# First quarter of a fused attention and feed-forward kernel: block widths 480, 512, 512, 416, single weight issues, tile 0 in three pieces, engine orders written out

## Chip, cores and metric

The kernel runs on one core of a Trainium2 chip. The metric is the device time of one execution in microseconds (us), the median over several runs. The profiler's times count from the first instruction of the program.

## What is computed

x has 2048 rows of 640 numbers, all in float32. Each row is normalised; from it come an attention branch, with 32 heads of 20 over a window of 8 positions two apart, and a feed-forward branch of width 1536.

```python
xn = _layernorm(x)                                  # x: (1, 2048, 640)
qkv = (xn @ wqkv).reshape(B, S, 3, 32, 20)          # wqkv: (640, 1920)
idx = pos[:, None] - off[None, :]                   # off = arange(8) * 2
logits = einsum("bhsd,bhswd->bhsw", q, k[idx]) * 20 ** -0.5   # masked where idx < 0
s = einsum("bhsw,bhswd->bhsd", softmax(logits), v[idx]).reshape(B, S, 640) @ wo
g = silu(silu(xn @ w1) @ w2)                        # w1: (640, 1536), w2: (1536, 640)
out = x + s * g
```

## The kernel before

The 2048 rows are worked on in four groups of 512 (half of the sequence, even or odd rows), each of four tiles of 128 rows. For every group TensorE runs the QKV product, then (from the second group on) the output projection of the group before, then the feed-forward part; after the last group comes its output projection. To keep float32 accuracy every operand is split into a high part, rounded to the matmul's float32r, and a low part, the remainder; a product of a 128-row slice is three matmuls: high by high, low by high, high by low. In the code these are TH and TL for the activations, and wh and wl for the weights; a product (k, c) is k = 0 for TH by wh, 1 for TL by wh, 2 for TH by wl, on the 128-row slice c of 5.

The QKV columns (1920) are worked on in four blocks, called quarters after their eight heads: block q has BQ = 192 columns of Q (64 in the last) beside 160 of K and 160 of V, so 512, 512, 512 and 384 columns. A block for a group is 5 slices by 4 tiles by 3 matmuls, 60 in all. Blocks 2 to 4 and all later groups go slice by slice over the four tiles (L735 to L749). The first block of the first group is special, since nothing is loaded then: `first_quarter` (L629) writes its order out by hand. It warms TensorE up with 22 transposes of the identity, and then interleaves, tile by tile, the turning of x (`turn`, transposes on TensorE, high part on ACT, low part on DVE) with lists of products (`products`). `begin` (L640) makes the statistics of a tile (two halves, an aggregate), the root on ACT (L461), the reciprocal (L463) and the scaling (L652), which for tile 0 is cut in two pieces of 384 and 256 columns.

Weights come by `raw_load` (L360), which for a QKV block issues two DMAs, the Q columns (L384) and the K and V columns (L385), on the queue of SyncE (SP). `w_load` (L397) splits them: the high part on ACT (L418, here called wh0 for block 0 of the weight units, and so on), the low part on GpSimd or, for the units named in ON_DVE, on DVE (L421, wl0 and so on). The split halves go to a ring of seven slots (WR) and are also stored to DRAM (L427), from where later groups load them again (L410). x tile t is loaded by `load_x` (L447); the first tile comes in two halves (L693).

Each engine runs its instructions in the order in which the program has them. That order is made by a planner, the class Weave: every operation is added with an engine, a duration, what it reads and writes, and a priority; `order` (L139) simulates the engines with these durations and takes, for each engine but TensorE, the ready operation that can start first, by priority among equals. TensorE's order is that of the program text. The planner has constants for the landing of a DMA (LAND, EARLY, RATE), for the load of an activation table (TABLE), and a rule, `held_back` (L115), by which ACT puts off an operation that would delay a silu that is due. SP's order in the start follows priorities: the weight unit k has 1 + k, and the tiles 1 to 3 of x have X_AT.

## Time and profile before

| | us |
|---|---|
| median of 3 runs | 619.84 (619.4 to 620.7) |
| the profiled execution | 619.89 |
| its span, first to last instruction | 618.1 |
| TensorE busy in the span | 612.7 (99%) |
| VectorE (DVE) busy | 561.5 (91%) |
| ScalarE (ACT) busy | 309.1 (50%) |
| GpSimd (POOL) busy | 112.6 (18%) |

The page gives the busy time of each engine, the chain of work that ended last and the costliest groups of instructions; PE is TensorE's matmuls and PEld its weight loads, which overlap them. A matmul's duration in the trace includes its way through the array, so that the rate of a row of matmuls is read from their starts, or from a stretch that holds a known number of them. What the numbers of the rows mean is said where they are used.

### The profile page before, as it was taken

The page shows a single profiled execution, that of the slowest core. Times are in us where ns is not written, and L with a number is a line of the kernel's source. Part 1 is how long each engine was busy: PE and PEld are TensorE (multiplying, and loading weights), DVE is VectorE, ACT ScalarE, POOL GpSimd, SP SyncE. Part 2 cuts the span into 40 slices and gives each one's busy share as a digit, 9 for nine tenths or more (in the row PEclk, how much of TensorE's full clock was granted, in tenths as well). Part 3 has the DMA queues.
Part 4 walks back from the last instruction along what each step waited for, and adds up shares of the span by engine and source line. Part 5 has one row for each costly group of instructions (what it writes and reads, how often), then busy time and mean ns, then how long its engine had stood idle before and what let it go on. Part 6 is the DMA issues. An engine that isn't in the chain of part 4 may idle for free.

```text
span 618.1 us, 9090 instructions
## 1 busy us (share of the span) xinstructions
PE 612.7 (99%) x3357; PEld 553.6 (90%) x3357; DVE 561.5 (91%) x581; ACT 309.1 (50%) x651; POOL 112.6 (18%) x168
## 2 busy tenths in 40 slices
PE   8999999999999999999999999999999999999997
PEld 7889899998889999999888999999988999999997
DVE  6558999999989998999998999999979999899974
ACT  5435548937376313951944502583396316153650
POOL 4510000011101133111222233311121213311100
PEclk9999999999999999999999999999999999999999
DMA  8999999875999998764699999955579999966642
GB/s 254 339 282 332 368 355 394 331 239 178 296 325 350 343 357 256 240 195 142 190 254 244 332 338 308 281 180 163 160 204 283 245 327 289 309 192 197 206 131 105
DMA packets 65449, 162.45 MB, mean 263 GB/s; under 512 B 7053, under 2 KB 29165, under 8 KB 65405
## 3 DMA queue, kind: packets, MB, share of 16 engines
q0 software_dynamic: 20016, 82.58, 44.3%
q1 hardware_dynamic: 45389, 79.29, 40.7%
q8 instruction: 26, 0.43, 0.3%
q14 instruction: 18, 0.15, 0.1%
HBM read 109.55 MB, written 34.16 MB: 232 GB/s over the span
## 4 chain that ended last, share of the span: by engine, by line
PE 99%; DVE 0%; ACT 0%; issue 0%; POOL 0%; POOLq 0%
PE acc L774 22%; PE acc L777 15%; PE acc L746 10%; PE acc L745 10%; PE acc L747 10%; PE rot L894 9%; PE rot L895 9%; PE rot L893 9%; PE acc L684 2%; PE rot L635 1%; PE rot L777 1%; PE rot L774 0%; PE rot L662 0%; PE acc L875 0%; ACT w L418 0%
## 5 line engine op out<-in xcount | busy, mean ns | idle before, releaser
L747 PE MATMUL acc<-w,thl 128*128 128x512 f32 (+1 forms) x300 | 112.4, 375 | 0.0
L746 PE MATMUL acc<-w,thl 128*128 128x512 f32 (+1 forms) x300 | 112.4, 375 | 0.0
L745 PE MATMUL acc<-w,thl 128*128 128x512 f32 (+1 forms) x300 | 112.4, 375 | 0.0
L774 PE MATMUL acc<-w,sh 128*128 128x384 f32 x384 | 111.7, 334 | 0.0
L777 PE MATMUL acc<-w,sh 128*128 128x256 f32 x384 | 107.1, 279 | 0.0
L899 ACT ACTIVATE sh<-rot 128x512 fp32r<-128x512 f32 x48 | 28.7, 597 | 155.6 <-PE rot L895 155.4
L895 PE MATMUL rot<-thl,w 128*128 128x512 f32 x240 | 93.8, 391 | 0.0
L894 PE MATMUL rot<-thl,w 128*128 128x512 f32 x240 | 93.8, 391 | 0.0
L893 PE MATMUL rot<-thl,w 128*128 128x512 f32 x240 | 93.5, 389 | 0.0
L579 DVE TENSOR_TENSOR pr<-q,kv 128x2560 f32<-128x2560 f32 x32 | 90.2, 2817 | 1.3 <-DMA kv<-kv 1.1
L617 DVE TENSOR_TENSOR pr<-e,kv 128x2560 f32<-128x2560 f32 x32 | 90.3, 2823 | 0.7
L582 DVE TENSOR_REDUCE l<-pr 128x128 f32<-128x2560 f32 x32 | 90.0, 2813 | 0.5
L622 DVE TENSOR_TENSOR pr<-pr 128x1280 f32<-128x1280 f32 x64 | 74.0, 1156 | 1.5
L774 PEld LDWEIGHTS acc<-w,sh 128*128 128x128 f32 x384 | 72.1, 188 | 1.1
L777 PEld LDWEIGHTS acc<-w,sh 128*128 128x128 f32 x384 | 72.2, 188 | 0.9
L410 POOL DMA_DIRECT2D w<-half_w x72 | 38.5, 534 | 189.1 <-PE acc L777 64.4
L410 POOL DMA_DIRECT2D w<-half_q x52 | 27.6, 531 | 238.8 <-DVE thl L480 91.0
L745 PEld LDWEIGHTS acc<-w,thl 128*128 128x128 f32 x300 | 56.3, 188 | 8.7
L747 PEld LDWEIGHTS acc<-w,thl 128*128 128x128 f32 x300 | 56.3, 188 | 8.7
L746 PEld LDWEIGHTS acc<-w,thl 128*128 128x128 f32 x300 | 56.3, 188 | 8.6
L774 PE MATMUL acc<-w,thl 128*128 128x384 f32 x225 | 63.1, 333 | 0.0
L495 ACT ACTIVATE xin<-sf 32x256 f32<-32x256 f32 (+1 forms) x144 | 54.6, 379 | 9.6 <-DVE sf L522 7.9
(92 smaller groups left out, 1044.5 us busy)
## 6 DMA issues: line engine op xcount, KB each, us to landing
w<-half_w POOLq DMA_DIRECT2D x72, 640.0 KB, 6.2
w<-half_q POOLq DMA_DIRECT2D x39, 512.0 KB, 4.6
half_w<-w SPq DMA_DIRECT2D x24, 640.0 KB
w<-half_wo POOLq DMA_DIRECT2D x15, 640.0 KB, 5.6
kv<-kv SPq DMA_DIRECT2D x15, 560.0 KB
half_q<-w SPq DMA_DIRECT2D x15, 512.0 KB
kv<-kv SPq DMA_DIRECT2D x15, 420.0 KB
gate<-in_B_w_dram SPq DMA_DIRECT2D x16, 320.0 KB
```

Source lines behind the costliest of these rows:

```text
L579: dve(2560, lambda t=t: nc.vector.tensor_tensor(out=PR, in0=win(qq[:, t:t + 2, :], W, 0), in1=win(kv[:, 0, t:t + 2, :], W, CQ), op=OP.mult ...
L582: dve(2560, lambda t=t: nc.vector.tensor_reduce(out=l[:, t:t + 2].rearrange("p t w h -> p (t w h)"), in_=PR.rearrange("p t w (h d) -> p (t ...
L617: dve(2560, lambda t=t, v=v: nc.vector.tensor_tensor(out=PR.rearrange("p t w (h d) -> p t (w h) d", d=DH), in0=e[:, t:t + 2].rearrange("p ...
L622: dve(2 * k * CQ, lambda k=k: nc.vector.tensor_tensor(out=PR[:, :, 0:k, :], in0=PR[:, :, 0:k, :], in1=PR[:, :, k:2 * k, :], op=OP.add), [] ...
L745: nc.tensor.matmul(o, hi, wh, start=c == 0, stop=False)
L746: nc.tensor.matmul(o, lo, wh, start=False, stop=False)
L747: nc.tensor.matmul(o, hi, wl, start=False, stop=c == DC - 1)
L774: nc.tensor.matmul(a[t][0][:, :CA], st, w[:, :CA], start=first, stop=last)
L777: nc.tensor.matmul(b[t // 2][0][:, h * CB:(h + 1) * CB], st, w[:, CA:], start=first and h == 0, stop=last, skip_group_check=True)
L893: nc.tensor.matmul(h, wh[:, cs], TH[i][:, c, :], start=c == 0, stop=False)
L894: nc.tensor.matmul(h, wh[:, cs], TL[i][:, c, :], start=False, stop=False)
L895: nc.tensor.matmul(h, wl[:, cs], TH[i][:, c, :], start=False, stop=c == DC - 1)
```

## The change

The Q columns are cut 160, 192, 192, 96, so that the blocks have 480, 512, 512 and 416 columns. A block of the first quarter then has three equal pieces of 160 columns and comes by one DMA in place of two. A pair of halves of under 512 columns is laid out with the second half at column 512, and its store and loads name the two halves. Tile 0 of x is scaled and turned in pieces of one, two and two slices. The warm-up has 18 transposes. The lists of products are written in one string, FIRST, and orders for ACT, DVE and GpSimd in ORDER; `chain` makes each named operation of an engine wait in the plan for the one before it (a name that stands under an engine which does not run it is passed over). In FIRST, T is a turn, with the pieces if any are named; 0h1 is tile 0, high by high, slice 1; x is low by high, and w high by low. In ORDER, q and r are a tile's root and reciprocal, s its statistics, g its aggregate, a its scaling, h and l its high and low parts (tile, piece). The subtractions for the weight units 0, 3 and 8 are on DVE, where 2, 3 and 4 were. Tiles 1 to 3 of x get the places 2.5, 4.5 and 6.5 among the weight units. The planner's landing times for early DMAs are changed, and `held_back` counts a table load also for operations without a table when the loaded table is not silu's.

```diff
-BQ = 192
+QC = 160, 192, 192, 96
+QO = 0, 160, 352, 544
+PAIR = 512
-WARM, WARM2 = 22, 3
+WARM, WARM2 = 18, 3
-X_AT = 2, 7, 8
-TILE_AT = 1, 1.5, 2, 2.5
+X_AT = 2.5, 4.5, 6.5
-ON_DVE = (2, 3, 4)
+ON_DVE = (0, 3, 8)
+FIRST = """T00 T01 0h0 T02 0h1 0x0 0x1 0h2 0h3 0x2 0w1 0w2 T1 0w0 0x3 0x4 1h0 0h4 1h2 1h34 0w4 0w3 1x0
+           1x1 1x2 1w3 1w4 1x4 T2 1w01 1x3 2w0 1h1 2h4 2h3 2w1 1w2 2h01 2h2 T3 2x0 2x123 2w3 3w012 2w4
+           3h4 3w34 3h0123 3x01234 2w2 2x4"""
+ORDER = {"ACT": """q0 wh0 wh1 h00 h01 wh2 h02 wh3 q1 wh4 h10 h11 q2 h20 h21 q3 h30 h31 wh5""",
+         "DVE": """wl2 s0a s0b g0 r0 a00 a01 a02 s1b s1a l00 l01 g1 l02 r1 a10 wl3 s2b s2a l10 g2 s3a
+                   l11 r2 a20 s3b g3 r3 a30 l20 l21 l31 l30""",
+         "POOL": """wl1 wl0 wl4 wl5"""}
...
-    EARLY = 10.0, 0.6
+    EARLY = 5.5, 1.45
...
                 if o.table is not None and o.table != "silu":
                     need += self.TABLE * (1 + (o.table != table)) + (self.GATE if gate else 0)
+                elif table != "silu":
+                    need += self.TABLE
...
+    def chain(self):
+
+        for e, names in ORDER.items():
+            row = [self.named[n] for n in names.split() if n in self.named and self.named[n].eng == e]
+            for a, b in zip(row, row[1:]):
+                a.users.append(b)
+                b.left += 1
+
     def order(self):
+        self.chain()
...
-                o.end = dma + self.LAND + o.late + (self.EARLY[1] if lanes[e][-1] and t < self.EARLY[0] else 0.0)
+                o.end = dma + (self.EARLY[1] if t < self.EARLY[0] else self.LAND) + o.late
...
     def width(u):
-        return qcols(u[1]) + 2 * CQ if u[0] == "q" else D
+        return QC[u[1]] + 2 * CQ if u[0] == "q" else D
...
+    def both_of(r, n):
+        if n < PAIR:
+            return r[:, :2 * PAIR].rearrange("p (k m) -> p k m", k=2)[:, :, :n]
+        return r[:, :2 * n].rearrange("p (k m) -> p k m", k=2)
...
             def go():
-                nc.sync.dma_start(r[:, :w], all3[:, 0, q * BQ:q * BQ + w])
+                if w == CQ:
+                    nc.sync.dma_start(r.rearrange("p (s m) -> p s m", s=3), all3[:, :, q * CQ:(q + 1) * CQ])
+                    return
+                nc.sync.dma_start(r[:, :w], all3[:, 0, QO[q]:QO[q] + w])
                 nc.sync.dma_start(r[:, w:].rearrange("p (s m) -> p s m", s=2), all3[:, 1:, q * CQ:(q + 1) * CQ])
...
-            add("POOL", 1.0, lambda: nc.gpsimd.dma_start(both, src), [("half", u)], [kh, kl], due + 10,
+            add("POOL", 1.0, lambda: nc.gpsimd.dma_start(both, src.rearrange("p (k m) -> p k m", k=2)), [("half", u)], [kh, kl], due + 10,
...
-        PARTS = (0, 3), (3, DC)
+        PARTS = ((0, 1), (1, 3), (3, DC)), ((0, 3), (3, DC))
...
-        turn(0)
-        pe(0.11 * WARM2, lambda: warm(WARM2, ACC[5]), [], [("acc", 5)])
-        products(0, [(0, 0), (1, 0), (0, 1), (1, 1), (2, 0), (0, 2), (1, 2)])
-        turn(1)
-        products(0, [(2, 1), (0, 3), (1, 3), (2, 2)])
-        products(1, [(0, 0), (0, 1), (0, 2)])
...
+        for step in FIRST.split():
+            if step[0] == "T":
+                turn(int(step[1]), [int(j) for j in step[2:]] or (0, 1))
+                turned[0] = 1
+                continue
+            t, k, cs = int(step[0]), "hxw".index(step[1]), step[2:]
+            products(t, [(k, int(c)) for c in cs], 0.1 * turned.pop(0))
```

## Rows read from the trace of the kernel before

**Rows 1.** The page: busy time, share, count by engine; the chain's shares by engine.
```profile
PE 612.7 (99%) x3357; PEld 553.6 (90%) x3357; DVE 561.5 (91%) x581; ACT 309.1 (50%) x651; POOL 112.6 (18%) x168
...
PE 99%; DVE 0%; ACT 0%; issue 0%; POOL 0%; POOLq 0%
```
**Rows 2.** Waits of TensorE, whole span: for whom, us in total, times, longest.
```profile
PE rot L635 <- POOL ident masks.py:199: 1.4, 1, 1.4
PE acc L684 <- ACT w L418: 0.2, 1, 0.2
```
**Rows 3.** Busy by stretch: us, PE PEld DVE ACT POOL, clock, DMA share, GB/s.
```profile
24.00:37.60 13.60, 13.60 (x61) 11.26 (x60) 7.92 (x16) 4.87 (x12) 8.92 (x6) 1.00 1.04 287
...
51.20:61.60 10.40, 10.40 (x61) 10.40 (x60) 8.77 (x10) 6.28 (x14) 0.00 (x0) 1.00 1.07 367
```
**Rows 4.** Timeline of TensorE's matmuls: start, duration, engine, line, operation, shapes, count.
```profile
7.46 1.89 PE L684 MATMUL acc<-w,thl 128*128 128x512 f32 x5
...
10.12 0.75 PE L662 MATMUL rot<-ident,xin 128*128 128x128 f32 x5
10.62 4.81 PE L684 MATMUL acc<-w,thl 128*128 128x512 f32 x20
...
24.00 0.39 PE L745 MATMUL acc<-w,thl 128*128 128x512 f32 x1
```
**Rows 5.** Timeline of TensorE's weight loads for the warm-up transposes.
```profile
1.38 4.55 PEld L635 LDWEIGHTS rot<-ident 128*128 128x128 f32 x22 [1.38 <-POOL ident masks.py:199]
...
6.83 0.36 PEld L635 LDWEIGHTS acc<-ident 128*128 128x128 f32 x3
```
**Rows 6.** Timeline of DVE in the first quarter; in brackets idle time and releaser.
```profile
4.84 0.80 DVE L652 TENSOR_SCALAR xin<-xin,mv,sd 128x384 f32<-128x384 f32 x2
6.26 0.49 DVE L647 BATCH_NORM_STATS2 st<-xin 128x6 f32<-128x320 f32 x1 [0.61 <-DMA xin<-in_A_x_dram]
7.44 0.56 DVE L670 TENSOR_TENSOR thl<-rot,thl 128x384 fp32r<-128x384 f32 x1 [0.69 <-ACT thl L666]
...
9.21 0.83 DVE L652 TENSOR_SCALAR xin<-xin,mv,sd 128x640 f32<-128x640 f32 x1
...
12.61 0.88 DVE L647 BATCH_NORM_STATS2 st<-xin 128x6 f32<-128x320 f32 x2
...
14.62 0.61 DVE L652 TENSOR_SCALAR xin<-xin,mv,sd 128x640 f32<-128x640 f32 x1
```
**Rows 7.** The same timeline, ACT and GpSimd.
```profile
6.19 1.27 POOL L421 TENSOR_TENSOR w<-pr,w 128x512 fp32r<-128x512 f32 x1 [2.97 <-ACT w L418]
...
8.68 0.29 ACT L461 ACTIVATE sd<-mv,epst 128x1 f32<-128x1 f32 x1 [0.34 <-DVE mv L648]
```
**Rows 8.** The same timeline, issues on SP's queue.
```profile
1.67 0.43 SPq L384 DMA_DIRECT2D pr<-in_A_wqkv_dram  x1
...
2.62 0.47 SPq L447 DMA_DIRECT2D xin<-in_A_x_dram  x1
```
**Rows 9.** Busy by stretch before 7.46; the last two columns are DMA share, GB/s.
```profile
1.40:3.25 1.85, 1.85 (x9) 1.85 (x10) 0.22 (x3) 0.84 (x2) 1.82 (x1) 1.00 0.64 195
3.25:4.50 1.25, 1.25 (x8) 1.25 (x7) 1.00 (x3) 0.18 (x1) 0.00 (x0) 1.00 0.67 148
4.50:5.90 1.40, 1.40 (x8) 1.40 (x7) 0.96 (x3) 0.53 (x2) 0.00 (x0) 1.00 1.04 352
5.90:7.46 1.56, 1.53 (x11) 1.29 (x9) 0.51 (x2) 0.75 (x3) 1.27 (x1) 1.00 1.01 280
```
**Rows 10.** The page: a costly group (mean ns) and DMA issues (us to landing).
```profile
L617 DVE TENSOR_TENSOR pr<-e,kv 128x2560 f32<-128x2560 f32 x32 | 90.3, 2823 | 0.7
...
w<-half_q POOLq DMA_DIRECT2D x39, 512.0 KB, 4.6
```
**Rows 11.** Timelines of DVE and of TensorE's weight loads at the last projection's start.
```profile
598.63 1.29 DVE L480 TENSOR_TENSOR thl<-xin,thl 128x512 fp32r<-128x512 f32 x2 [2.22 <-ACT thl L479]
...
600.97 0.19 PEld L774 LDWEIGHTS rot<-w,thl 128*128 128x128 f32 x1
```

More of the change, by code (lines that the diff above doesn't have):

```diff
@@ L59 @@
 class Op:
-    __slots__ = ("eng", "dur", "fn", "prio", "lock", "table", "nbytes", "late", "seq", "left", "users", "ready", "start", "end")
+    __slots__ = ("eng", "dur", "fn", "prio", "lock", "table", "nbytes", "late", "seq", "left", "users", "ready", "start", "end", "lag")
 class Weave:
@@ L84, in __init__, with add @@
         self.writer, self.readers = {}, {}
-    def add(self, eng, dur, fn, reads=(), writes=(), prio=0.0, lock=False, table=None, nbytes=0, late=0.0):
+        self.named = {}
+    def add(self, eng, dur, fn, reads=(), writes=(), prio=0.0, lock=False, table=None, nbytes=0, late=0.0, name=None, lag=0.0):
         o = Op()
-        o.late = late
+        o.late, o.lag = late, lag
+        if name:
+            self.named[name] = o
         o.eng, o.dur, o.fn, o.prio, o.lock, o.table, o.nbytes = eng, dur, fn, prio, lock, table, nbytes
@@ L198, in order @@
                 u.left -= 1
-                hop = self.HOP if u.eng != e or o.nbytes else 0.0
+                hop = self.HOP if u.eng != e or o.nbytes else -o.lag
                 if u.eng == "ACT" and e == "DVE" and u.prio > 0:
@@ L294, in local_attention_silu_ffn, with dve, act, pe @@
     po = lambda n: 0.11 + n * 0.0023
-    def dve(n, fn, reads, writes, prio, lock=False):
-        add("DVE", dv(n), fn, reads, writes, prio, lock)
-    def act(n, fn, reads, writes, prio, table=None):
-        add("ACT", ac(n), fn, reads, writes, prio, table=table)
-    def pe(dur, fn, reads, writes):
-        add("PE", dur, fn, reads, writes)
+    def dve(n, fn, reads, writes, prio, lock=False, name=None):
+        add("DVE", dv(n), fn, reads, writes, prio, lock, name=name)
+    def act(n, fn, reads, writes, prio, table=None, name=None):
+        lag = 0.09 if name else 0.0
+        add("ACT", ac(n) - lag, fn, reads, writes, prio, table=table, name=name, lag=lag)
+    def pe(dur, fn, reads, writes, lag=0.0):
+        add("PE", dur, fn, reads, writes, lag=lag)
         clock[0] += dur
@@ L404, in w_load @@
         r = WR[s]
-        both = r[:, :2 * n]
+        both = both_of(r, n)
         kh, kl = ("wh", s), ("wl", s)
@@ L421, in w_load @@
         add(eng, cost, lambda: by.tensor_tensor(
-            out=r[:, n:2 * n], in0=raw, in1=r[:, :n].bitcast(F32), op=OP.subtract), [kh] + kr, [kl],
-            due if pool_does else LOW_AT if k < LO else 50, lock=True)
+            out=both[:, 1], in0=raw, in1=r[:, :n].bitcast(F32), op=OP.subtract), [kh] + kr, [kl],
+            due if pool_does else LOW_AT if k < LO else 50, lock=True, name=f"wl{k}")
         if what[i] == "store":
@@ L426, in w_load @@
             halves[u] = kept
-            dma(lambda: nc.sync.dma_start(kept, both.bitcast(F32)), [kh, kl], [("half", u)], 2 * n * P * 4,
+            dma(lambda: nc.sync.dma_start(kept.rearrange("p (k m) -> p k m", k=2), both.bitcast(F32)), [kh, kl], [("half", u)], 2 * n * P * 4,
                 due + STORE)
@@ L438, in w_next @@
         s, n = i % RING, width(want)
-        return WR[s][:, :n], WR[s][:, n:2 * n], ("wh", s), ("wl", s)
+        both = both_of(WR[s], n)
+        return both[:, 0], both[:, 1], ("wh", s), ("wl", s)
     def w_done(n=1):
@@ L448, in load_x @@
             [("xin", u) for u in range(t, t + n)], n * P * D * 4, clock[0] if prio is None else prio,
-            late=LATE if g else 0.4 * t)
+            late=LATE if g else 0.0)
     def ln_stats(t, after=()):
@@ L457, in ln_stats, with ln_rstd @@
         dve(60, lambda: nc.vector.bn_aggr(out=MV[:, t, :], in_=st), [ks + (0,), ks + (1,)], [("mv", t)], 1)
-    def ln_rstd(a, b, at=1, after=()):
+    def ln_rstd(a, b, at=1, after=(), name=None):
         n = range(a, b)
         act(b - a, lambda: nc.scalar.activation(SD[:, 0, a:b], MV[:, a:b, 1], AF.Sqrt, bias=epst, scale=1.0),
-            [("mv", t) for t in n] + list(after), [("sd", t) for t in n], 0, "sqrt")
+            [("mv", t) for t in n] + list(after), [("sd", t) for t in n], 0, "sqrt", name=name and "q" + name)
         dve(10, lambda: nc.vector.reciprocal(out=SD[:, 1, a:b], in_=SD[:, 0, a:b]),
-            [("sd", t) for t in n], [("rs", t) for t in n], at)
+            [("sd", t) for t in n], [("rs", t) for t in n], at, name=name and "r" + name)
     def ln_apply(t):
@@ L671, in turn, with products @@
                     out=TL[i][:, a:b, tsl(t)], in0=v, in1=TH[i][:, a:b, tsl(t)].bitcast(F32), op=OP.subtract),
-                    [kp] + t_keys(i, range(a, b), [t], ["th"]), t_keys(i, range(a, b), [t], ["tl"]),
-                    1.6 if a and not t else 0)
-        def products(t, steps):
+                    [kp] + t_keys(i, range(a, b), [t], ["th"]), t_keys(i, range(a, b), [t], ["tl"]), 0, name=f"l{t}{j}")
+        def products(t, steps, more):
             o, kp = ps[t]
@@ L683, in products @@
                 given[t] = given.get(t, 0) + 1
-                pe(mm(512), lambda x=x, c=c, w=w, first=first, last=last: nc.tensor.matmul(
-                    o, x[i][:, c, tsl(t)], w, start=first, stop=last), [(kx, i, c, t), kw], [kp])
-        def passes(*ks):
-            return [(k, c) for k in ks for c in range(DC)]
+                pe(mm(480) + more, lambda x=x, c=c, w=w, first=first, last=last: nc.tensor.matmul(
+                    o[:, :w.shape[1]], x[i][:, c, tsl(t)], w, start=first, stop=last), [(kx, i, c, t), kw], [kp])
+                more = 0.0
         given = {}
```

63 lines of the change are left out of this document (29 added, 34 removed).

## The prediction

> **What bounds the kernel now.** First read the busy shares and the chain on the page: TensorE is busy 99% of the span, and the chain that ended last is TensorE throughout [rows 1]. Then ask what TensorE waited for: in the whole span the list has two waits, 1.4 us for the identity at the start and 0.2 us for a weight split, and nothing later [rows 2]. Then see what a matmul costs where nothing waits: 60 matmuls of 512 columns take 13.60 us (0.2267 each), 60 of 384 take 10.40 (0.1733 each) [rows 3]. The difference is 0.0534 us for 128 columns, so 0.0133 for 32. From 24.00 on the kernel is a string of such matmuls without a gap; that part can only change with its columns, or get a new wait. So the change must earn its time before 24.00, in the first quarter [rows 4]: tile 0's first product starts at 7.46, seven products are done by 10.12, where tile 1's transposes begin, and from there 53 products and 15 transposes run almost closed to 24.00: 10.12 + 53 x 0.2267 + 3 groups of transposes at 0.50 (10.12 to 10.62) = 23.63, which leaves 0.37 for small gaps.
>
> So the end of the kernel hangs on two numbers: when tile 1's transposes start (T1, now 10.12), and how many products are done by then.
>
> **The profiled execution** took 619.89 us with a span of 618.1; the median of the three runs is 619.84. I count within the span and carry the sum to the median; the two stand 0.05 apart.
>
> **Widths.** In groups 1 to 3, 60 products of 480 gain 60 x 0.0133 = 0.80 us and 60 of 416 give it back: nil. In group 0 the last block pays the same 0.80, but the first quarter earns only on what runs behind T1, as products before it lie beside waits: 51 x 0.0133 = 0.68. Net 0.12 slower. 480 and 416 lie between measured widths, so I take them on their line. A reader who looks at the first quarter alone books 0.7 us that the last block takes back.
>
> **One issue per weight block.** A block of the first quarter is two issues on SP's queue; two of them take it from 1.67 to 2.62 [rows 8]. With one, five steps of 0.47 fall away, 2.3 us of queue, and the x tiles move past weights on it: x1 goes behind blocks 0 and 1 (was behind 0), x2 behind 3 (was behind 5), x3 behind 5 (was behind 6). The queue then has x1 at 2.6 as now, x2 near 4.0, block 4 near 4.5. But an issue is not a landing. The DMA engines are busy 0.67 of 3.25 to 4.50, at 148 GB/s, and full from 4.50 on, at 352 and then 280 GB/s [rows 9]. Only the first stretch had room: filling it gives (148/0.67 - 148) x 1.25 = 91 KB, or at 280 GB/s 165 KB. Moved by 5.90 are 195 x 1.85 + 148 x 1.25 + 352 x 1.40 = 1039 KB, so 1130 to 1204 with the change. How far use lags behind: x1 is used at 6.26 [rows 6], when 1039 + 0.36 x 280 = 1140 KB had moved; up to and with x1, 917 KB were asked for; the lag is 223 KB. In the new order x1 stands at 1145 KB, block 2 at 1390, block 3 at 1635, block 4 at 2208 (245 KB a block, 328 a tile). At 280 GB/s from 5.90: x1 at 6.5 to 6.8, block 2 at 7.4 to 7.6, block 3 at 8.2 to 8.5, block 4 at 10.3 to 10.6. Bounds: with 352 GB/s held, x1 6.4, block 3 7.8, block 4 9.4; with nothing gained, 7.1, 8.8 and 10.9. I take 7.4, 8.3 and 10.3 for the blocks.
>
> The Trainium skill, page "DMA: Bandwidth & Descriptors", section "Issuing engines are not separate DMA queues", says that the sequencer time saved on issuing is usually small beside the transfer itself. From 4.50 on the trace agrees, from 3.25 to 4.50 (0.67) it does not. By that rule alone the issues saved would be worth nothing: the third case below.
>
> **Orders of DVE and ACT up to T1.** T1 needs x1, its two statistics, the aggregate, the root on ACT (q1), the reciprocal and the scaling (a10). Now the second statistic waits behind tile 0's subtraction of 7.44, the root comes at 8.68, right behind the aggregate, the scaling at 9.21 to 10.04 [rows 6, 7]. The new DVE order has both statistics first (0.88 for such a pair at 12.61), then the subtractions l00 and l01, 0.25 and 0.42 by the 0.56 of 384 columns: the aggregate is done 1.8 us behind x1, at 8.5. But the new ACT order has q1 behind the split of block 3, and this split waits for its landing: 8.3 + 0.55 = 8.85. From root to T1 there are 10.12 - 8.68 = 1.44 us, with a scaling of 0.83; the same scaling took 0.61 at 14.62, so T1 comes 1.22 to 1.44 behind 8.85, at 10.07 to 10.29; with block 3 at its bounds, 9.6 and 10.8. I take the low end, 10.0.
>
> Queued behind q1 on ACT are the split of block 4 and then h10, tile 1's high half. Block 4 at 10.3 puts h10's end near 11.3; TensorE comes to its product 1h0 at T1 + 0.50 + 3 x 0.2133 = 11.1. This new wait costs 0.2; with block 4 at its bounds, 0 and 0.5.
>
> Subtractions change engines: blocks 0 and 3 on DVE, 1, 2 and 4 on GpSimd, at 1.27 each [rows 7]. Block 2 at 7.4 is split by 8.0 and subtracted by 9.3; its product is the last before T1 and ends at 9.6. That is 0.4 of cover; with block 2 at 8.0 the cover is gone and T1 0.2 later. Block 0's, now on DVE without a fixed place, is wanted only behind T1; ahead of the scaling it would cost up to 0.6. I take 0.
>
> **Three pieces of tile 0, warm-up of 18.** The scaling starts at 4.84 as now, in three pieces; the warm-up ends 0.85 earlier, so the first transpose can go near 5.25 and the first product near 6.4, against 7.46. That gives room for nine products before T1, against seven: 2 x 0.2267 = 0.45 us that is no longer run behind it. The earlier start gives nothing besides: 0x0 needs l00 (7.7), and the queue is in order.
>
> The clock: the weight loads of the 22 warm-up transposes come every 0.207 us, those of the three at 6.83 every 0.12 [rows 5]: the lower level (1.2 GHz), then the higher (2.4), though the clock column of [rows 3] says 1.00. TensorE had run without a gap until then; in the new kernel it has gaps from 5.3 to 6.4. If the rise comes later but before T1, the four products behind block 3's split take 0.2 more each: 0 to 0.8. I take 0.
>
> The skill's page "TensorE: Matmul & The Clock Gate", Part 4, has it that transposes do not release the clock. Here it rose after nothing but transposes. By the rule the four cut ones could not matter, by the trace they could.
>
> **Layout and planner.** Stored blocks of 480 and 416 become two runs in place of one. Such loads land 4.6 us after issue [rows 10], seven slots of 2.7 us ahead; doubled it would be hidden still: 0. The rule that holds ACT's copies back for a table load can move any copy of the later groups; ACT is busy 50% [rows 1]. No wait of TensorE there can go, as there is none: 0, or the last rival.
>
> **Sum.** T1 0.12 earlier, two products 0.45, widths -0.12, h10 -0.2, and 0.15 of the 0.37 of gaps, as x2 and x3 come some 3 us sooner (tile 2's statistics are at 12.61 now): 0.4 us. 619.84 - 0.4 = **619.4**. Its own range: T1 at 9.6 and no wait, 0.52 + 0.45 - 0.12 + 0.15 = 1.0, 618.8; T1 at 10.7 and a wait of 0.5, 0.6 slower, 620.4.
>
> **The rivals.** Larger gain, **618.3** (617.9 to 618.6): single issues hold 352 GB/s, block 3 lands by 7.5, q1 goes right behind the aggregate (8.1), T1 is at 9.3, h10 does not wait, the gaps are gone: 0.82 + 0.45 - 0.12 + 0.37 = 1.5. For it: the engines reached that rate once [rows 9]; against it: they were full at 280 afterwards. Chance 0.22.
>
> Nothing gained, **619.9** (619.6 to 620.3): issue was no bound, block 3 comes at 8.8, T1 at 10.5; the two products make good what that costs: -0.38 + 0.45 - 0.12. For it: share 1.01 at 5.90 [rows 9]; against it: the idle third before. Chance 0.12.
>
> Slower, **621.2** (620.3 to 622.5): the later groups are planned anew and the last join breaks. The last two subtractions of the turned attention output run from 598.63 to 599.92; the weight load that needs the second stands at 600.97 [rows 11], 1.05 us of room. DVE is busy 91% [rows 1]. One of its 2.8 us operations [rows 10] put ahead of that chain leaves TensorE standing 2.8 - 1.05 = 1.75 us: less 0.4, 1.35 slower. It decides once the chain comes 1.05 us later against TensorE. Against it: the chain follows TensorE's own results, so a common shift leaves the room. Chance 0.13.
>
> **How the numbers follow.** Forecast 0.53, rivals 0.22, 0.12 and 0.13. A measurement of this kernel can tell about 0.2%, 1.24 us, from no change: faster is below 618.60, slower above 621.08. Faster takes the larger gain and 0.03 of the forecast's edge, 0.25; slower takes 0.08 of the last rival and 0.02 of a late clock, 0.10; the same has 0.65. The range, 618.0 to 621.0, leaves out some 0.07 below and 0.11 above.
>
> **What would show it.** The second quarter's first product near 22.8 (24.00 now); group 0's last block 11.2 us long (10.40 now); T1 near 10.0, behind block 3's split and q1 on ACT; h10 behind block 4's split. T1 before 9.5 shows the larger gain, a wait of TensorE after 24 the last rival, products spaced 0.4 apart after 7.5 the late clock. Wrong from the ground would be blocks of 480 and 416 off the line of [rows 3].

## The result and the profile after

The changed kernel takes 622.68 us (median of 20 runs, 620.47 to 623.66), the kernel before 619.82 (20 runs, 619.26 to 623.40): ratio 1.0033 [1.0023, 1.0043], slower by 0.33% or 2.1 us (the ratio goes by the means; the medians lie 2.9 apart), where 0.4 us faster was forecast and 621.0 was the top of the range. The profiled execution of after took 623.66 us with a span of 621.9, against 619.89 and 618.1; it is the slowest of its twenty. Executions of one kernel lie up to 4 us apart here, so verdicts come from ratios with their intervals, and single profiles are asked for mechanisms.

TensorE's timeline of after, to be held against [rows 4] (start, duration, what it waited for in brackets):

```profile
6.75 0.48 PE L715 MATMUL acc<-w,thl 128*128 128x480 f32 x1 [0.75 <-ACT thl L698]
...
7.21 0.46 PE L715 MATMUL acc<-w,thl 128*128 128x480 f32 x1
9.32 3.17 PE L715 MATMUL acc<-w,thl 128*128 128x480 f32 x7 [1.65 <-DVE thl L702]
12.29 1.27 PE L694 MATMUL rot<-ident,xin 128*128 128x128 f32 x5
...
26.46 0.40 PE L770 MATMUL acc<-w,thl 128*128 128x512 f32 x1
```

The first product comes 0.7 sooner than before, nine are done ahead of tile 1's transposes as planned, and yet T1 is at 12.29 (10.12 before) and the second quarter at 26.46 (24.00). Busy by stretch, columns as in [rows 3] (the granted clock is the third from the end):

```profile
7.70:9.30 1.60, 0.00 (x0) 0.00 (x0) 1.11 (x4) 0.41 (x1) 0.13 (x1) 0.78 1.08 368
9.30:12.29 2.99, 2.97 (x8) 2.35 (x9) 2.58 (x8) 1.78 (x5) 1.61 (x2) 0.50 1.08 338
12.29:17.70 5.41, 5.41 (x22) 4.76 (x21) 3.04 (x10) 2.14 (x6) 0.81 (x1) 0.71 0.96 295
17.70:26.50 8.80, 8.80 (x48) 7.60 (x46) 2.46 (x6) 4.08 (x12) 2.96 (x3) 1.00 1.01 314
...
53.71:64.91 11.20, 11.20 (x61) 11.18 (x60) 10.69 (x13) 7.30 (x16) 0.00 (x0) 1.00 1.06 329
147.30:160.30 13.00, 13.00 (x62) 11.25 (x61) 12.90 (x10) 12.43 (x30) 1.60 (x3) 1.00 0.68 196
160.30:173.90 13.60, 13.60 (x61) 11.25 (x60) 13.39 (x13) 5.41 (x14) 1.76 (x3) 1.00 1.04 351
```

Two things are to be seen. TensorE stands idle from 7.70 to 9.30, the clock falls, and the products up to T1 run at half of it (the lower level, 1.2 GHz), 0.4 us apart. And 60 products of 480 columns take 13.00 us, not the 12.80 of the line; 416 take 11.20, as on it. The span's 3.8 us are then accounted for: 26.46 - 24.00 = 2.46 in the first quarter, 11.20 - 10.40 = 0.80 in group 0's last block, and three times 13.00 + 11.20 - 13.60 - 10.40 = 0.20 in groups 1 to 3, together 3.86. The last term is the roughest: from block start to block start it is 0.12 a group, and elsewhere the later groups move by up to 0.4 us either way, which nearly cancels. TensorE has one later wait, the second of these, at a feed-forward product:

```profile
PE acc L715 <- DVE thl L702: 1.6, 1, 1.6
...
PE acc L799 <- DVE sl L926: 0.2, 1, 0.2
```

DVE and ACT say why 0x0 starts at 9.32. Tile 0's low part (L702) stands behind tile 1's statistics (L674) in the written order, and these wait 1.71 us for tile 1's x:

```profile
8.19 0.89 DVE L674 BATCH_NORM_STATS2 st<-xin 128x6 f32<-128x320 f32 x2 [1.71 <-DMA xin<-in_A_x_dram]
8.99 0.60 DVE L702 TENSOR_TENSOR thl<-rot,thl 128x128 fp32r<-128x128 f32 x2
...
10.71 0.61 DVE L680 TENSOR_SCALAR xin<-xin,mv,sd 128x640 f32<-128x640 f32 x1
...
9.69 0.60 ACT L445 ACTIVATE w<-pr 128x480 fp32r<-128x480 f32 x1
10.20 0.28 ACT L489 ACTIVATE sd<-mv,epst 128x1 f32<-128x1 f32 x1
```

### The profile page after: what moved, and what is told of

It reads as the page before. It is cut to its first block, busy times and chain, and to the rows that moved or that the text cites. A ratio compares the mean times of both kernels' runs of the same rounds, so it can differ in the third digit from the quotient of the medians.

```text
span 621.9 us, 9064 instructions
## 1 busy us (share of the span) xinstructions
PE 614.4 (99%) x3350; PEld 557.2 (90%) x3350; DVE 563.1 (91%) x583; ACT 309.4 (50%) x652; POOL 117.6 (19%) x168
## 4 chain that ended last, share of the span: by engine, by line
PE 95%; DMA 2%; DVE 1%; POOL 1%; SPq 0%; issue 0%; POOLq 0%
PE acc L799 21%; PE acc L802 14%; PE acc L772 10%; PE acc L771 10%; PE acc L770 10%; PE rot L919 8%; PE rot L920 8%; PE rot L918 8%; PE acc L715 2%; DMA xin<-in_A_x_dram 1%; DMA xr<-in_A_x_dram 1%; POOL xr L847 1%; DVE pr L607 1%; PE rot L802 1%; DMA out_dram<-xr 0%; PE rot L799 0%
## 5 line engine op out<-in xcount | busy, mean ns | idle before, releaser
L772 PE MATMUL acc<-w,thl 128*128 128x512 f32 (+2 forms) x300 | 112.9, 376 | 0.0
L771 PE MATMUL acc<-w,thl 128*128 128x512 f32 (+2 forms) x300 | 112.9, 376 | 0.0
L770 PE MATMUL acc<-w,thl 128*128 128x512 f32 (+2 forms) x300 | 112.8, 376 | 0.0
L799 PE MATMUL acc<-w,sh 128*128 128x384 f32 x384 | 111.5, 333 | 0.0
L645 DVE TENSOR_TENSOR pr<-e,kv 128x2560 f32<-128x2560 f32 x32 | 92.0, 2875 | 0.8
L607 DVE TENSOR_TENSOR pr<-q,kv 128x2560 f32<-128x2560 f32 x32 | 91.5, 2859 | 0.5 <-DMA gate<-in_A_wqkv_dram 0.4
L650 DVE TENSOR_TENSOR pr<-pr 128x1280 f32<-128x1280 f32 x64 | 78.4, 1225 | 1.4
L437 POOL DMA_DIRECT2D w<-half_q x52 | 32.7, 629 | 234.2 <-ACT w L445 92.8
L799 PEld LDWEIGHTS acc<-w,sh 128*128 128x128 f32 x384 | 72.1, 188 | 0.9
L799 PE MATMUL acc<-w,thl 128*128 128x384 f32 x225 | 63.1, 333 | 0.0
```

Source lines behind the costliest of these rows:

```text
L607: dve(2560, lambda t=t: nc.vector.tensor_tensor(out=PR, in0=win(qq[:, t:t + 2, :], W, 0), in1=win(kv[:, 0, t:t + 2, :], W, CQ), op=OP.mult ...
L645: dve(2560, lambda t=t, v=v: nc.vector.tensor_tensor(out=PR.rearrange("p t w (h d) -> p t (w h) d", d=DH), in0=e[:, t:t + 2].rearrange("p ...
L650: dve(2 * k * CQ, lambda k=k: nc.vector.tensor_tensor(out=PR[:, :, 0:k, :], in0=PR[:, :, 0:k, :], in1=PR[:, :, k:2 * k, :], op=OP.add), [] ...
L770: nc.tensor.matmul(o, hi, wh, start=c == 0, stop=False)
L771: nc.tensor.matmul(o, lo, wh, start=False, stop=False)
L772: nc.tensor.matmul(o, hi, wl, start=False, stop=c == DC - 1)
```

## The experiments

Three theories at the start. **A**: tile 1's x lands late, the written orders hand its lateness to 0x0, and the idle time lets the clock fall. **B**: 480 columns are off the line, so the widths cost by themselves. **C**: the later groups are planned anew and get waits.

**Tile 0's low part first.**

```diff
-"DVE": ... a02 s1b s1a l00 l01 g1 l02 r1 a10 ...
+"DVE": ... a02 l00 l01 s1b s1a g1 l02 r1 a10 ...
```

> The changed kernel with one move in DVE's written order: tile 0's subtractions l00 and l01 stand ahead of tile 1's two statistics instead of behind them. Theory A (the time is lost in the first quarter: l00 waits behind statistics that wait for x1, TensorE stands still, and its clock falls for that): l00 runs near 6.9 instead of 8.99, the standing of 1.7 us before 0x0 shrinks under 0.7, the granted clock does not fall or falls for less, T1 comes near 10.5 instead of 12.29, the second quarter starts near 23.7 instead of 26.46, and the time is 620.0 (619.5 to 620.7), some 2.5 below the changed kernel. Theory B (the widths cost it): T1 may come sooner, but at least 0.8 of the loss stays. Theory C (the later groups, planned anew, cost it): no gain over 0.5, 622.2 or more.

Measured: 621.95 us, ratio 1.0014 [1.0001, 1.0027]. TensorE no longer waits for l00, but 1.4 us for the split of block 2, and the clock still fell, later:

```profile
9.50 0.49 PE L715 MATMUL acc<-w,thl 128*128 128x480 f32 x1 [1.36 <-ACT w L445]
...
11.00:14.60 3.60, 3.60 (x14) 2.96 (x13) 3.38 (x10) 2.23 (x5) 1.38 (x2) 0.53 0.93 268
```

Part of A: the order cost something, but the blocks are the next to be late.

**Transposes in the gap** (16 of the identity between 0h1 and 0x0).

```diff
-WARM, WARM2 = 18, 3
+WARM, WARM2 = 18, 16
-FIRST = T00 T01 0h0 T02 0h1 0x0 0x1 ...
+FIRST = T00 T01 0h0 T02 0h1 W 0x0 0x1 ...
```

> The changed kernel with 16 more transposes of the identity (1.8 us of TensorE at the higher clock) put into the place where TensorE stands, between 0h1 and 0x0; nothing else is moved. It tells the price of the wait from the price of the clock. Theory A with the clock as its larger part: the granted clock stays at the higher level from its first rise on, 0x0 still starts near 9.3, but the products behind it come every 0.217 instead of 0.400, T1 near 11.4, second quarter near 24.1, time 620.3 (619.8 to 621.2). Theory A with the wait alone: 0 to 0.4 gained. Theories B and C: nothing gained, 622.2 to 623.

Measured: 622.75, ratio 1.0035 [1.0024, 1.0047].

```profile
9.24 1.78 PE L715 MATMUL acc<-w,thl 128*128 128x480 f32 x7
...
23.67 0.40 PE L770 MATMUL acc<-w,thl 128*128 128x512 f32 x1
```

In its profile 0x0 starts at 9.24, as late as in after, but the clock held and the second quarter starts at 23.67, 2.8 sooner. So in these two profiles most of what the quarter lost came from the half clock behind the gap, and not from the gap's own length. The total did not follow: there are 1.0 us in two new waits at L799 (theory C), and the profiled execution is the fastest of its twelve (622.03 to 624.11).

**Widths alone**, on the kernel before.

```diff
-BQ = 192
+QC = 160, 192, 192, 96
+QO = 0, 160, 352, 544
```

> The kernel before with the widths of 480, 512, 512 and 416 columns alone: two issues for each block, the orders, the places of x and the warm-up of the kernel before. Theory B (products of 480 columns come every 0.2165 us, not 0.2133 as their line has it): last block of group 0 0.8 longer, first quarter 53 x 0.0102 = 0.54 shorter, groups 1 to 3 each 60 x 0.0032 = 0.19 longer: 0.83 slower than before, 620.6 (620.3 to 621.0). With 480 on the line: 0.12 slower, 619.9. Theory A alone says 0 to 0.2 slower; theory C that a plan made anew by the other durations alone gives waits of TensorE behind 24, visible as such.

Measured: 621.41, ratio 1.0012 [0.9999, 1.0024]. The second quarter starts at 23.20, 0.80 sooner; group 0's last block and groups 1 to 3 take back 0.80 and 0.60 by the stretches. That is theory B. But 0.45 of the 0.80 lie in T1, which the widths do not explain (10.12 before):

```profile
9.67 0.76 PE L667 MATMUL rot<-ident,xin 128*128 128x128 f32 x5
```

**Tile 1 sooner in the changed kernel.**

```diff
-X_AT = 2.5, 4.5, 6.5
+X_AT = 1.5, 4.5, 6.5
```

> The changed kernel with x1 put behind weight block 0 on SP's queue instead of behind block 1 (place 1.5 instead of 2.5), all other orders as they are. Theory A: x1 is issued near 2.4 instead of 3.08 and lands 0.5 to 0.7 sooner (7.5 to 7.7 instead of 8.17); l00, which waits behind its statistics, comes as much sooner, but block 1 and with it h00 and the first product come 0.5 later; the standing before 0x0 shrinks from 1.65 to about 0.6, the time falls by 0.5 to 2 according to the clock: 620.5 to 622.2. Theories B and C: no change over 0.3.

Measured: 622.79, ratio 1.0036 [1.0021, 1.0051]. Block 1 now lands behind tile 1, and ACT's written order has its split ahead of tile 0's high part:

```profile
8.73 0.77 PE L715 MATMUL acc<-w,thl 128*128 128x480 f32 x1 [2.54 <-ACT thl L698]
```

A miss of A as I had put it: the orders hold for one sequence of landings, and another sequence meets another wait. The clock is part of the loss here too, by a late rise: eight products start between 9.58 and 12.92, 0.4 us apart, the lower level; the trace's first record of the higher one is at 14.28.

```profile
9.58:12.92 3.34, 3.34 (x10) 2.68 (x9) 2.26 (x4) 1.62 (x4) 2.66 (x3) 1.00 1.09 338
```

The clock column says 1.00 for them, as it does for the slow warm-up in [rows 9], and the mean of this execution is 0.999. So column and mean show a fall of the clock, but not a first rise that comes late.

**The loads of before under the new orders**, with the new widths and then with the old.

```diff
-                if w == CQ:
-                    nc.sync.dma_start(r.rearrange("p (s m) -> p s m", s=3), all3[:, :, q * CQ:(q + 1) * CQ])
-                    return
-X_AT = 2.5, 4.5, 6.5
+X_AT = 2, 7, 8
```

and for the old widths also

```diff
-QC = 160, 192, 192, 96
+QC = 192, 192, 192, 64
```

> The changed kernel with the loading of before: every block of the first quarter by two issues again, tile 1 issued behind the first block (X_AT 2, 7, 8). Widths, pieces, warm-up of 18 and written orders stay. Theory A (tile 1 comes late because an issue in three pieces holds SP 0.61 to 0.71 us, and the low part of tile 0 is written behind tile 1's statistics): tile 1 lands near 6.3, as in the run with the widths alone, the product 0x0 starts by 8.1 and not at 9.32, tile 1's transposes by 11.0, the second quarter by 24.6 where the clock holds; ratio to before about 1.0012 (what the widths cost alone). Rival L (the loads are not the matter, the written orders and the pieces are): the second quarter stays at 25.5 or later, ratio 1.0025 or more.

> The run before this one with the blocks of before too (512, 512, 512, 384 columns): what is left of the change is the pieces, the warm-up of 18 and the written orders. If these are neutral or better once tile 1 lands early: second quarter between 23.6 and 24.4, ratio 0.9993 to 1.0006. If they cost by themselves (tile 0's low part behind tile 1's statistics, a clock that falls more easily): second quarter at 25 or later, ratio 1.0015 or more. Against the run with two issues and the new widths it tells the price of the widths a second time: 0.6 to 1.0 us by theory B.

Measured: 621.86, 1.0029 [1.0020, 1.0037], and 621.41, 1.0023 [1.0013, 1.0032]. Both first products wait over 2 us for the same ACT order (8.12 and 8.23, [2.15 and 2.03 <-ACT thl]), so neither isolates the loads. The pair puts the widths at 0.0006, which its intervals cannot tell from nothing.

**A warm-up of 24 transposes.**

```diff
-WARM, WARM2 = 18, 3
+WARM, WARM2 = 24, 3
```

> The changed kernel with a warm-up of 24 transposes in place of 18. Theory A with the clock: the idle time of TensorE that lets the clock fall is that of 5.3 to 6.7 together with that of 7.7 to 9.3; six more transposes fill up to 0.6 us of the first (1.3 at half clock), so the clock holds more often, the median drops by 0.5 to 1.5 us (621.2 to 622.2) and the second quarter starts near 25.0 where it holds. Rival: the warm-up changes nothing, because the idle time of 7.7 to 9.3 is what lets it fall; then 622.7 within 0.4, and if the transposes reach past the landing of tile 0's first part, up to 0.4 slower.

Measured: 621.58 (621.04 to 622.13), ratio 1.0019 [1.0007, 1.0030]. The mean granted clock was 0.999 or 1.000 in all 12 executions; in 12 of 20 of after it was 0.997 or less. The median of those twelve is 622.7 and that of the other eight 622.2 (620.5 to 623.4), so the mean does not sort the executions of after; some of the eight may have had a late rise, which it would not show. The profile, with a stretch's clock:

```profile
10.74 0.77 PE L694 MATMUL rot<-ident,xin 128*128 128x128 f32 x5
...
15.60 0.76 PE L694 MATMUL rot<-ident,xin 128*128 128x128 f32 x5 [0.63 <-DVE xin L680]
...
24.34 0.39 PE L770 MATMUL acc<-w,thl 128*128 128x512 f32 x1
...
9.30:12.29 2.99, 2.93 (x16) 2.06 (x15) 2.68 (x7) 1.91 (x5) 1.78 (x2) 1.00 1.10 344
```

T1 is at 10.74, the second quarter at 24.34, 2.1 sooner than in after's profile; the ratios lie 0.0014 apart, 0.9 us, and their intervals overlap. The clock is not all of that: the first product comes 0.6 later and tile 1's statistics start at 7.49, not 8.19, so TensorE stands 0.36 us ahead of 0x0 and not 1.65.

**The pitch by width**: 60 products in a row of each width, behind the end of the kernel before.

```diff
+        for n in widths:
+            for c in range(DC):
+                for t in range(T):
+                    for x, off in ((OH, 0), (OL, 0), (OH, lo)):
+                        nc.tensor.matmul(ACC[t][:, :n], x[1 - slot][:, c, tsl(t)], WR[c][:, off:off + n],
+                                         start=c == 0 and x is OH and not off, stop=c == DC - 1 and off > 0)
```

> The kernel before, and behind its end 660 products that no output takes: 60 in a row of 384, 416, 448, 464, 480, 496 and 512 columns, 480 and 512 once more, then 480 and 448 with the low part 480 columns behind the high part. On the line of the prediction 60 of them take 10.40, 11.20, 12.00, 12.40, 12.80, 13.20 and 13.60 us. If the width of 480 itself is off the line, as the 13.00 of groups 1 to 3 of the changed kernel say (theory B), 480 takes 13.00 here too and 416 takes 11.20; if it is the place of the low part, 480 takes 12.80 in one of the two places; if it is other work beside them in the kernel, 12.80 in both. The kernel's own part takes what before takes, the whole some 135 us more.

```profile
614.72:625.12 10.40, 10.40 (x63) 10.40 (x62) 0.85 (x2) 0.00 (x0) 0.00 (x0) 1.00 0.10 33
625.12:636.32 11.20, 11.20 (x62) 11.20 (x61) 0.00 (x0) 0.00 (x0) 0.00 (x0) 1.00 0.00 0
636.32:648.45 12.13, 12.13 (x61) 11.25 (x61) 0.00 (x0) 0.00 (x0) 0.00 (x0) 1.00 0.01 1
648.45:661.25 12.80, 12.80 (x61) 11.23 (x60) 0.00 (x0) 0.00 (x0) 0.00 (x0) 1.00 0.00 0
661.25:674.21 12.96, 12.96 (x61) 11.26 (x60) 0.00 (x0) 0.00 (x0) 0.00 (x0) 1.00 0.01 1
...
687.81:701.81 14.00, 14.00 (x61) 11.22 (x60) 0.00 (x0) 0.00 (x0) 0.00 (x0) 1.00 0.01 1
...
728.77:741.77 13.00, 13.00 (x61) 11.29 (x60) 0.00 (x0) 0.00 (x0) 0.00 (x0) 1.00 0.00 0
```

In order: 384, 416, 448, 464, 480, 512, and 480 with the low part 480 columns behind. 480 takes 12.96 to 13.00 wherever its low part lies and with no other engine at work: it is the width (B). The time rises unevenly and not on a line; why 512 takes 14.00 here and 13.60 in the kernel stays open (its low part lies 640 columns behind the high part here, 512 there; no run tells whether that is why).

**Both repairs of A**: low part first and 24 transposes.

> The changed kernel with both repairs of theory A at once: tile 0's low parts (l00, l01) written ahead of tile 1's statistics, and a warm-up of 24. If the late x1 in front of l00 and the clock are all that its first quarter lost, the clock holds as with 24 transposes alone, 0x0 starts right behind 0h1 near 8.0, tile 1's transposes lie between 10.2 and 10.9 (now by tile 1's own landing at 7.5 to 8.2 and its chain of some 2.7 us), the second quarter starts at 23.8 to 24.4; ratio to before 1.0012 to 1.0020, 0.2 us better than with 24 transposes alone. Rival: the chain of tile 1 (landing, statistics, normalizing) is what ends last, and moving l00 ahead of it only shifts the wait from 0x0 to tile 1's transposes: nothing gained against 24 alone, 1.0019.

Measured: 622.09, ratio 1.0029 [1.0013, 1.0045]; T1 at 10.86, the second quarter at 24.44. The rival: the wait only moves, to block 2 (0.93 us ahead of 0h2 at 9.06).

**The loads of before with ACT's order mended**, 24 transposes; with the new and the old widths.

```diff
-"ACT": q0 wh0 wh1 h00 h01 wh2 ...
+"ACT": q0 wh0 h00 h01 wh1 wh2 ...
```

> The run with two issues an block (loads of before, tile 1 behind the first block) with the split of block 1 on ACT moved behind h00 and h01, and a warm-up of 24. There block 1 landed at 7.22, and ACT held h00 behind its split (2.1 us of TensorE). If that place alone spoiled it, the first product now starts near 7.4, tile 1 is normalized by 9.5, tile 1's transposes start by 10.4, the second quarter by 23.7, the clock holds; ratio 1.0008 to 1.0014, that is better than the single issues with the same warm-up (1.0019). If the single issues are the better loads after all (blocks 3 and 4 land a microsecond sooner), the second quarter is at 24.3 or later and the ratio 1.0018 or more.

> The run before this one with the blocks of before (512, 512, 512, 384): pieces, written orders and warm-up of 24 on the loads and widths of before. If the widths cost 0.6 to 1.0 us (theory B) it is that much faster than the run before it, though its second quarter starts up to 0.8 later (23.9 to 24.5); ratio 0.9992 to 1.0004. If it is no faster than that run, the widths cost nothing and theory B falls. Under 0.9990 the pieces and orders are worth something once the clock holds, and this is faster than both kernels.

Measured: 623.42, 1.0050 [1.0035, 1.0065], and 620.85, 1.0010 [1.0000, 1.0020]. Both misses. With the new widths the plan of the later groups puts a weight split that waits for its load ahead of an eviction on ACT (theory C), 1.5 of the 3.1 us that the ratio gives:

```profile
PE acc L770 <- ACT q L564: 1.5, 1, 1.5
...
53.25 0.74 ACT L445 ACTIVATE w<-gate 128x640 fp32r<-128x640 f32 x1 [4.99 <-DMA gate<-in_B_w_dram]
```

With the old, DVE's written order has a statistic of tile 3 ahead of tile 1's low part, and with the loads of before tile 3 lands later; TensorE stands 0.8 us for that low part:

```profile
15.10 0.49 DVE L674 BATCH_NORM_STATS2 st<-xin 128x6 f32<-128x320 f32 x1 [1.33 <-DMA xin<-in_A_x_dram]
15.51 0.41 DVE L702 TENSOR_TENSOR thl<-rot,thl 128x256 fp32r<-128x256 f32 x1
```

**Single issues alone**: the widths run and one issue per block, tile 1 still behind the first; no written orders, pieces or shorter warm-up.

```diff
+                if w == CQ:
+                    nc.sync.dma_start(r.rearrange("p (s m) -> p s m", s=3), all3[:, :, q * CQ:(q + 1) * CQ])
+                    return
```

> The kernel before with the new widths, and the first quarter's blocks by one issue each, tile 1 still behind the first block; no written orders, no pieces, warm-up of 22. If the single issue brings the blocks sooner, as the prediction had it (0.47 a step), blocks 2 and 3 land 0.3 to 0.8 sooner than 8.26 and 9.01, and the second quarter starts at 22.4 to 23.0, where the widths alone had 23.20; ratio 1.0000 to 1.0010. If the transfers and not the issues set the landings (blocks 2 and 3 at 8.24 and 9.02 in the run with 24 transposes), nothing is gained: second quarter 23.2 to 23.6, ratio 1.0010 to 1.0020. If it harms by itself, 24 or later, 1.0025 and more.

Measured: 620.52, ratio 1.0006 [0.9995, 1.0018]; no wait of TensorE behind the identity's.

```profile
9.74 0.77 PE L670 MATMUL rot<-ident,xin 128*128 128x128 f32 x5
...
23.07 0.39 PE L753 MATMUL acc<-w,thl 128*128 128x512 f32 x1
...
6.46 0.89 DVE L655 BATCH_NORM_STATS2 st<-xin 128x6 f32<-128x320 f32 x2 [0.81 <-DMA xin<-in_A_x_dram]
```

The second quarter starts 0.13 sooner than with two issues, and the ratios can't be told apart: no gain and no harm of the single issues is seen.

**The same with tile 1 behind two blocks**, its place in the changed kernel.

```diff
-X_AT = 2, 7, 8
+X_AT = 2.5, 7, 8
```

> The run with widths and single issues alone (no written orders, no pieces, warm-up of 22; second quarter at 23.07, ratio 1.0006), with one thing changed: tile 1 is issued behind two blocks, as in the changed kernel, and not behind one. If tile 1's place in the loads is what its first quarter lost, tile 1 lands near 7.5 (there 6.4), its transposes start 0.8 to 1.2 later (10.5 to 10.9, there 9.74), the second quarter at 23.7 to 24.4, ratio 1.0015 to 1.0030. If the loads' order is harmless and the written orders with the nine products are the cause, the second quarter stays within 0.3 of 23.07, ratio 1.0002 to 1.0012.

Measured: 621.60, ratio 1.0024 [1.0011, 1.0036]; T1 1.00 later, the second quarter at 23.96, 0.89 later.

```profile
7.97 0.89 DVE L655 BATCH_NORM_STATS2 st<-xin 128x6 f32<-128x320 f32 x2 [0.54 <-DMA xin<-in_A_x_dram]
...
10.74 0.77 PE L670 MATMUL rot<-ident,xin 128*128 128x128 f32 x5 [0.71 <-DVE xin L660]
...
23.96 0.39 PE L753 MATMUL acc<-w,thl 128*128 128x512 f32 x1
```

With no written orders, pieces or shorter warm-up beside it, tile 1's place in the queue costs 0.89 us by the two profiles and 1.1 by the ratios, whose intervals just overlap.

**No written orders** in the changed kernel (ORDER empty).

> The changed kernel without the written orders (the table of orders is empty, the planner orders all engines again); TensorE's sequence, single issues, pieces, widths and the warm-up of 18 stay. The planner puts l00 ahead of tile 1's statistics and both statistics of tile 1 between the low parts, and block 6's split ahead of tile 2's square root. If the written orders are what the first quarter lost beside the clock, the second quarter starts at 23.5 to 24.8 and the ratio is 1.0012 to 1.0022. If the landings bind either way (tile 1 at 7.5 to 8.2, block 2 at 8.2 to 8.9), it stays at 1.0025 to 1.0040, as with the orders.

Measured: 624.40, ratio 1.0067 [1.0049, 1.0085], a miss of both: with TensorE's new sequence the planner's own orders are worse (the first product waits 1.4 us, a low part of a weight block 1.6), so the written ones are worth 0.0034 there. Half clock is part of both totals: here, too, the clock rose late (13.77), and the eight products from 8.50 to 12.08 run some 0.4 apart.

**The kernel before with 24 transposes.**

> The kernel before with a warm-up of 24 transposes in place of 22, everything else in the same order on every engine. Tile 0's transposes can start up to 0.43 later (two transposes at half clock). If the times of before above 621 come from a clock that falls or rises late in the first quarter, they go with 24, as the clock of 0.997 went in the changed kernel: 619.3 to 620.3 in all but one or two runs, ratio 0.9985 to 1.0000. If they have another origin, the tail stays and the ratio is 1.0000 to 1.0008.

Measured: 620.01 (619.34 to 621.88), ratio 1.0000 [0.9986, 1.0013]. The spread of before stays, so its cause is not the length of the warm-up, and it stays open; nor is this a better version.

**What the runs blamed, taken back at once**: 24 transposes, tile 1 behind the first block (X_AT 1.5), and

```diff
-"ACT": q0 wh0 wh1 h00 h01 wh2 h02 wh3 q1 wh4 h10 h11 q2 h20 ...
+"ACT": q0 wh0 h00 h01 wh1 wh2 h02 q1 wh3 wh4 h10 h11 q2 wh6 h20 ...
-"DVE": ... a02 s1b s1a l00 l01 g1 l02 r1 a10 ...
+"DVE": ... a02 s1b s1a g1 l00 l01 wl0 l02 r1 a10 ...
```

> The changed kernel with all that the runs blamed taken back: warm-up of 24, tile 1 issued behind the first block (X_AT 1.5), ACT's written order with h00 and h01 ahead of block 1's split and q1 ahead of block 3's, DVE's with tile 1's statistics closed (g1) ahead of l00. Single issues, pieces and widths stay. If the lateness of tile 1 and the fixed orders that wait on a block in front of tile 1's chain were the 1.1 us that the first quarter still lost with the clock held (24.34 against 23.20), tile 1 lands near 6.4, its transposes start by 10.1 and the second quarter by 23.6; ratio 1.0004 to 1.0014, no worse than the widths alone. If the nine products ahead of tile 1's transposes bind (0h3 needs block 3, which lands near 9.0 to 9.1 and is split by 9.8), tile 1's transposes stay at 10.4 or later and the second quarter at 23.9 or later, ratio 1.0012 to 1.0022.

Measured: 623.09, ratio 1.0063 [1.0039, 1.0088]. Tile 1 is used at 6.47, 1.7 sooner than in after, and T1 is at 11.51 all the same:

```profile
9.58 0.42 DVE L702 TENSOR_TENSOR thl<-acc,thl 128x256 fp32r<-128x256 f32 x1 [0.74 <-ACT thl L698]
...
10.11 1.34 DVE L680 TENSOR_SCALAR xin<-xin,mv,sd 128x640 f32<-128x640 f32 x1
...
8.40 2.70 POOL L448 TENSOR_TENSOR w<-pr,w 128x480 fp32r<-128x480 f32 x2 [5.17 <-ACT w L445]
```

l02 stands ahead of tile 1's reciprocal, and its high half on ACT behind the split of block 2; then the scaling takes 1.34 instead of 0.61. So a sooner tile 1 is lost to the orders around it, as far as T1 goes. The second quarter still starts at 24.26 (24.34 with 24 transposes), as tile 2's transposes wait for nothing here. So what makes this run slower than that one lies behind 24: 0.9 us are theory C again (an eviction behind a weight split, as above), and the rest of the 2.7 us between the two ratios stays open.

## Why the prediction was wrong

Set one above the other, the runs give the change in steps (start of the second quarter in each profile):

| kernel | ratio to before | second quarter |
|---|---|---|
| before | 1 | 24.00 |
| widths alone | 1.0012 [0.9999, 1.0024] | 23.20 |
| and single issues | 1.0006 [0.9995, 1.0018] | 23.07 |
| and tile 1 behind two blocks | 1.0024 [1.0011, 1.0036] | 23.96 |
| all of the change, 24 transposes | 1.0019 [1.0007, 1.0030] | 24.34 |
| the change | 1.0033 [1.0023, 1.0043] | 26.46 |

The intervals of neighbours overlap, and each start is that of one execution, so the sizes of the steps are rough, and by the ratios alone no single step is clear of noise.

**Widths: the step that failed is the line.** It gave nil for groups 1 to 3; they cost 0.60 by the stretches, 0.4 by block starts. Behind T1 the first quarter earned 0.35 (13.88 to 13.53 us), not 0.68; the 0.45 that T1 came sooner is no width's. The last block took 0.80 back, as put. In place of 0.12 the widths cost 0.4 by the spans of the two profiles, 0.85 by them without T1's share, and 0.74 by the ratio, whose interval just reaches 1. The prediction had named 480 off its line as what would make it wrong from the ground.

**One issue per block: the landings failed.** In after's profile tile 1 and blocks 3 and 4 are complete at 8.17, 9.66 and 11.19, where the latest bounds were 7.1, 8.8 and 10.9. An issue in three pieces holds SP for longer, and with two of them ahead tile 1 is issued at 3.08, not 2.6 (compare [rows 8]):

```profile
1.68 1.35 SPq L410 DMA_DIRECT2D pr<-in_A_wqkv_dram  x2
3.08 0.61 SPq L475 DMA_DIRECT2D xin<-in_A_x_dram  x1
```

The idle third of [rows 9] was not filled: from 3.25 to 4.50 the share is 0.68, as before (0.67).

```profile
1.40:3.25 1.85, 1.85 (x9) 1.85 (x10) 0.18 (x3) 0.84 (x2) 1.83 (x1) 1.00 0.59 177
3.25:4.50 1.25, 1.25 (x8) 1.25 (x7) 1.00 (x3) 0.18 (x1) 0.00 (x0) 1.00 0.68 187
4.50:5.90 1.40, 1.40 (x8) 0.92 (x6) 1.22 (x5) 0.72 (x2) 0.00 (x0) 1.00 1.09 334
```

177 x 1.85 + 187 x 1.25 + 334 x 1.40 = 1029 KB by 5.90, where 1130 to 1204 were forecast and 1039 measured before. Tile 1, moved behind a second block, is used at 8.19 (7.49 with 24 transposes, 7.97 in the run that changes its place alone), where 6.5 to 6.8 and at most 7.1 were forecast. Behind the late issue stands a larger part, which the sum by bytes left out. The trace shows tile 1's load completed in sixteen parts: eight are in by 6.61 and fourteen by 6.81, just as forecast, but the last two come at 8.04 and 8.17, and the statistics start behind the last. In all seven profiles with tile 1 behind two blocks of one issue each, eight are in by 6.6 to 6.9 and the last at 7.5 to 8.2; in before it is 5.91 and 6.24. So the lag taken from before held hardly any of this tail; what makes the tail longer here stays open.

The rival "nothing gained" had the reason, but its 7.1 for tile 1 is short as well, and it took block 3 alone on to T1. The rule of the Trainium skill that was cited there ("DMA: Bandwidth & Descriptors", "Issuing engines are not separate DMA queues") came true: by the single-issue run the sequencer time saved is worth nothing that can be measured.

**Orders.** That q1 goes behind the split of block 3 is seen (9.69, 10.20), and from the root to T1 it is 1.19 with 24 transposes (9.55 to 10.74), just under the 1.22 to 1.44. In after that chain does not end last: its scaling is done at 11.32, and TensorE is at its seven products of half clock until 12.29. But 0x0 was put at l00's 7.7, which is tile 1 at 6.8 and 0.88 for its statistics: with tile 1 at 8.19 it is 9.32. The step missed here is that l00, and 0x0 with it, stands behind tile 1's load and inherits its lateness; the range moved T1 with block 3 and left 0x0 where it was.

**Pieces and warm-up** did what was said: first product at 6.75 (forecast 6.4), nine products ahead of T1. The price lay beside them.

**The clock: a term of the sum, priced 0 with 0.8 as its end.** It cost 2.8 us in the pair of profiles in which 0x0 starts equally late (26.46 in after, 23.67 with transposes in the gap). By the ratios its price is not settled: 24 transposes are 0.9 us better than the change, within overlapping intervals, and the transposes in the gap are no better. The prediction looked only at a late rise ahead of T1 and counted four products; the trace of after shows a fall behind the idle stretch, and the half clock reaches past T1 over transposes and products up to about 15.4 (0.71 over 12.29 to 17.70: half for 0.58 of it). Against "TensorE: Matmul & The Clock Gate", Part 4, of the Trainium skill, the trace stays with [rows 5]: in the run with transposes in the gap, with nothing but transposes from 7.58 to 9.24, the products behind it ran at the higher level. The run with 24 transposes points the same way, but its gap was shorter too.

**Between 23.07 and 24.34**, with the clock held: T1 is 1.00 later, two products more are done by then (-0.43), and tile 2's transposes wait 0.63: 1.20 of 1.27. Those 0.63 are one scaling that took 1.29 in place of 0.61 (below). Whether pieces, sequence and orders together gain or lose, the ratios can't tell (1.0024, 1.0019).

**The last rival** forecast 621.2 by a new wait in the later groups. In the profile of the changed kernel it is 0.2, so this was not the cause there; in the profiles of four of the runs such waits cost 0.8 to 1.5, at an eviction or a feed-forward product, not at the last join that was named.

None of the runs beats both kernels.

## What to carry to other kernels

A written order fixes not only the engines but the landings it was made for: each wait for a DMA in it passes its lateness to everything behind, also to the engine whose order was left alone, so price every moved load by the time of its last part, at the first instruction that waits for it and at all that stand behind that one. Count an idle stretch of TensorE at the start with the half clock that may follow, not with its own length alone, and read the clock from the spacing of the products too, as the column misses a late first rise. And measure a new width before booking it between two known ones.
